# Sums of w_in in an earlier step, seven products in steps 5 and 18, and one filler less: a windowed attention and two-layer feed-forward kernel

## The chip, the core and the metric

The kernel runs on one core of one Trainium2 chip. The metric is the device time of an execution in microseconds (us); the number to be predicted is the median of the changed kernel's runs. A core has five engines with a queue each, worked in order: TensorE (PE: matmuls and, beside them, weight loads, PEld), VectorE (DVE), ScalarE (ACT), GpSimd (POOL) and SyncE (SP). They wait for each other by semaphores. Matmuls write to banks of PSUM, from where DVE or ACT take the results; everything else lies in SBUF. POOL issues the loads of q, k and v, SP the stores and the transposing DMAs.

## The reference

Eight batches and eight heads of 576 tokens with 64 channels: attention in a window of 32 tokens on either side, then a feed-forward block with a quick-GELU over all 4608 tokens of 512 channels.

```python
scores = scale * np.matmul(q, k.transpose(0, 1, 3, 2))
mask = np.abs(pos[:, None] - pos[None, :]) <= window          # window = 32
scores = np.where(mask, scores, -1000000000.0)
scores = scores - np.max(scores, axis=-1, keepdims=True)
attn = np.exp(scores)
attn = attn / (np.sum(attn, axis=-1, keepdims=True) + 1e-09)
attn_out = np.matmul(attn, v)
x = attn_out.transpose(0, 2, 1, 3).reshape(B * S, H * D)      # 4608 x 512
h = x @ w_in                                                  # 512 x 2048
g = h * (1.0 / (1.0 + np.exp(-1.702 * h)))
out = g @ w_out                                               # 2048 x 512
```

## The kernel before, in words

**Units and tiles.** The 4608 tokens, shifted by 32, are cut into 36 units of 128. For a unit u, `scores` makes the scores of 128 queries against the keys of their windows in 64 x 64 blocks (48 short matmuls) and lets ACT take the exponential; `band` multiplies with the 0/1 mask on DVE; `values` multiplies with v (and a column of ones, which gives the sums); `norm` divides on DVE; `x_T` transposes the result by a DMA on SP's queue into `xT`. Two units make a tile t of 256 tokens, `xT[t]`, on which the feed-forward block works.

**First layer, plain.** `layer1(t, d)` is a piece of two blocks of 128 of the 2048 hidden channels: 8 matmuls that stream 256 tokens each, into one bank, which ACT turns into `g` by its GELU. Eight pieces make the layer. A piece d above 3 covers blocks d and d + 8.

**First layer by seven products.** For half of the hidden channels (blocks 4 to 7 and 12 to 15) the product of a 2 x 2 block matrix can be made with seven block products instead of eight (Strassen's scheme in Winograd's form). `seven(t, n)` is one of them: 8 matmuls that stream 128 tokens each. It takes sums of blocks of x (`x_sums`, DVE) and of w_in (`w_in_sums`, DVE, made once), and collects in two banks, `h_main` and `h_side`; `move` copies or adds partial results between banks and SBUF (DVE or ACT), and `gelu` makes `g` of them.

**Second layer by seven products.** From tile 3 on g @ w_out goes the same way: `product(t, n)` is 8 matmuls that stream 256 columns, `g_sums` makes the sums of blocks of g (DVE), `w_sums` those of w_out (once, in the head). Products 1, 6, 7 and 4 add into one bank one after the other; after 1, 6 and 7 `keep` copies the running value to SBUF (DVE), and the next of them may not begin before. `result` adds the pieces to an output block, `store` sends it off.

**Order.** The program is an order written out by hand, engine queue by engine queue; nothing is reordered later, but for weight loads. It has five parts:

- `head`: loads, the first units, tiles 0 to 2. At its start PE gets *fillers*, matmuls on zeros whose result nobody reads (`keep_busy`). The number that is changed stands behind `blind(3)`, in front of the scores of units 2 and 3.
- `window(4)`: units 7, 8, 9, rest of the plain second layer, plain first layer of tile 3, all g sums of tile 3's first half, `feed(4)`.
- `window(5)`: units 10 and 11, products of tile 3, plain first layer of tile 4; at its end all g sums of tile 4's first half, `feed(5)`, the four w_in sums, and the last four pieces.
- `steady(w)` for w = 6 to 17: units 2w and 2w + 1, products of tile w - 2, first layer of tile w - 1 with four plain pieces and seven products. From w = 7 on, g sums 2 and 3 of a tile's first half are made in the step of its products (`if w > 6`).
- `window(18)` and `window(19)`, which go to `close`: no units are left. 18 interleaves the products of tile 16 with the plain first layer of tile 17; 19 has the products of tile 17 alone.

In the prediction "step w" is the part with that number. `loads(w)` stands at the head of a step and issues on POOL's queue the loads of v and of rows of q and k for later steps. `feed(w)` copies v for the odd blocks on DVE (`odd_v`), and issues four transposing DMAs of q and k rows (`rows_X`) on SP's queue. `gelu_table` brings ACT's table back to the GELU after the exponentials.

Banks: two of kind `h` (plain pieces; `h_main` and `h_side`), two of kind `b`, one each of `o` and `t`, and `a`, a pair of banks.

Of the kernel before, what the change touches and what calls it, by code (L numbers as in the profile page):

```python
# [15 lines left out]
F32 = mybir.dt.float32  # L16
# [11 lines left out]
class _Kernel:  # L28
# [454 lines left out]
    def head(self):  # L483

        nc, dve, act, pool = self.nc, self.nc.vector, self.nc.scalar, self.nc.gpsimd
# [55 lines left out]
        self.x_T(1, "o", dve)  # L541
        self.rest_T("q", "th", (dve, act))
        self.blind(3)
        self.keep_busy(2, "o")
        self.scores(2)
        self.scores(3)
        self.odd_v(2, dve)
# [23 lines left out]
        l2 = [(lambda c=c, u=u: self.layer2(u, c, "hhot"[u], (dve, act)[u % 2])) for c in range(4) for u in range(4)]  # L571

        def run(n):
            for _ in range(n):
                l2.pop(0)()

        run(4)
        for hp in range(4):
            self.rows_T("k", 1, hp, "b", dve)
            self.rows_T("q", 1, hp, "b", act)  # L580
            run(1)
        self.scores(4)
        self.scores(5)
        for m in range(4, 6):
            self.odd_v(m, dve)
        self.band(4)
        run(3)
        self.band(5)
        run(1)
# [43 lines left out]
        for c in "kq":  # L633
            self.rows_X(c, 3, (0, 1))

    def w_in_sums(self):

        w, ws, dve = self.w_in_sb, self.wi_sum, self.nc.vector
        top, low, u, v = slice(0, 2), slice(2, 4), slice(512, 1024), slice(1536, 2048)
        dve.tensor_add(ws[:, 0], w[:, top, v], w[:, low, v])  # L640
        dve.tensor_sub(ws[:, 1], ws[:, 0], w[:, top, u])
        dve.tensor_sub(ws[:, 2], w[:, top, u], w[:, top, v])
        dve.tensor_sub(ws[:, 3], w[:, low, u], ws[:, 1])

    def x_sums(self, t, which):

# [53 lines left out]
    def steady(self, w):  # L700

        dve, act = self.nc.vector, self.nc.scalar
        a, b, t, o = 2 * w, 2 * w + 1, w - 1, w - 2
        self.loads(w)
        self.scores(a, which=0)
        self.scores(b, which=1)
        self.g_sums(o, 1, (0, 1))
        self.product(o, 1, "o")
        self.keep(o, 1, dve)
        if w > 6:  # L710
            self.g_sums(o, 0, (2,))
        self.product(o, 2, "t")
        self.result(o, 11)
        self.gelu_table()
        self.product(o, 6)
        self.band(a)
        self.keep(o, 6, dve)
        self.product(o, 5, "t")
        self.band(b)
        self.g_sums(o, 1, (2,))  # L720
        self.seven(t, 1)
        self.move("side", "main", dve)
        self.x_sums(t, (0, 1))
        self.values(a, which=0)
        self.values(b, which=1)
        self.norm(a)
        self.x_T(a)
        self.product(o, 7)
        self.keep(o, 7, dve)
        self.result(o, 22)  # L730
        self.x_sums(t, (2, 3))
        self.norm(b)
        self.x_T(b)
        if w > 6:
            self.g_sums(o, 0, (3,))
        self.g_sums(o, 1, (3,))
        self.seven(t, 2)
        self.gelu(t, "side", 0, 0)
        self.seven(t, 6)
        self.move("k2", "main", act)  # L740
        self.layer1(t, 0, "a")
        self.product(o, 4)
        self.result(o, 21, act)
        self.seven(t, 7)
        self.move("k7", "side", act)
        self.seven(t, 5)
        self.move("22", "main", dve, "k7")
        self.feed(w)
        self.layer1(t, 1, "b")
        self.gelu(t, "22", 1, 1)  # L750
        self.layer1(t, 2, "b")
        self.layer1(t, 3, "a")
        self.seven(t, 4)
        self.move("21", "side", dve, "k2")
        self.seven(t, 3)
        self.gelu(t, "main", 0, 1)
        self.gelu(t, "21", 1, 0)
        self.g_sums(t, 0, (0, 1))
        self.product(o, 3)
        self.result(o, 12)  # L760

    def window(self, w):
        nc, dve, sp = self.nc, self.nc.vector, self.nc.sync
        a, b = 2 * w, 2 * w + 1
        att = w < self.NW
        t, act = w - 2, nc.scalar
        l1 = [(lambda d=d: self.layer1(w - 1, d)) for d in range(8)] if w <= self.NW else []

        def run(lst, n=1):
            for _ in range(min(n, len(lst))):  # L770
                lst.pop(0)()

        if w == 4:
            l2 = [(lambda u=u, i=i: self.layer2(u, i, "oh"[u % 2], (dve, act)[u % 2])) for u in (4, 5) for i in range(4)]
            self.scores(7)
            self.scores(a)
            run(l2, 3)
            self.band(7)
            self.scores(b)
            run(l2)  # L780
            self.band(a)
            self.values(7, "th")
            self.gelu_table()
            self.band(b)
            self.norm(7)
            run(l2, 2)
            self.values(a)
            self.values(b)
            run(l2)
            self.x_T(7, "t", nc.scalar)  # L790
            self.norm(a)
            self.x_T(a)
            self.norm(b)
            self.x_T(b)
            run(l2)
            self.loads(w)
            for m in (10, 11):
                self.odd_v(m, dve)
            run(l1, 8)
            self.g_sums(w - 1, 0)  # L800
            self.feed(w)
            return
        self.loads(w)
        if not att:
            self.close(w, l1)
            return
        self.scores(a, which=0)
        self.g_sums(t, 1, (0, 1))
        self.product(t, 1, "o")
        self.keep(t, 1, dve)  # L810
        self.product(t, 2, "h")
        self.scores(b, which=1)
        self.g_sums(t, 1, (2, 3))
        self.result(t, 11)
        self.gelu_table()
        self.product(t, 5, "t")
        self.band(a)
        self.product(t, 6)
        self.keep(t, 6, dve)
        self.band(b)  # L820
        run(l1)
        self.values(a, which=0)
        self.values(b, which=1)
        self.norm(a)
        self.x_T(a)
        self.product(t, 7)
        self.keep(t, 7, dve)
        self.result(t, 22)
        run(l1, 1)
        self.product(t, 4)  # L830
        self.result(t, 21, act)
        self.norm(b)
        self.x_T(b)
        self.product(t, 3)
        self.result(t, 12)
        run(l1, len(l1) - 4)
        self.g_sums(w - 1, 0)
        self.feed(w)
        self.w_in_sums()
        run(l1, 4)  # L840

    def close(self, w, l1):

        dve, act, t = self.nc.vector, self.nc.scalar, w - 2
        last = not l1
        if not last:
            self.g_sums(t, 0, (2, 3))
        self.g_sums(t, 1, (0, 1))
        for n, kind in ((1, "o"), (2, "b"), (6, None), (5, "b"), (7, None)):
            self.product(t, n, kind)  # L850
            if n in (1, 6, 7):
                self.keep(t, n, dve)
            if n == 1:
                self.g_sums(t, 1, (2, 3))
            if n == 2:
                self.result(t, 11)
            if l1:
                l1.pop(0)()
        self.result(t, 22)
        while len(l1) > 1:  # L860
            l1.pop(0)()
        if l1:
            self.g_sums(w - 1, 0)
        if not last:
            self.product(t, 4)
            self.result(t, 21, act)
            l1.pop(0)()
            self.product(t, 3)
            self.result(t, 12)
        else:  # L870
            both = self.work.tile([128, self.DM // 2], F32, name="part", tag="part", bufs=4)
            dve.tensor_add(both, self.part[t, "c"], self.part[t, 6])  # L872
            self.product(t, 3, "b")
            self.part[t, 6], self.part[t, "c"] = both, self.part[t, "d"]
            self.result(t, 12)
            self.product(t, 4)
            self.result(t, 21, act)

    def feed(self, w):

# [14 lines left out]

    def run(self):
        self.head()
        for w in range(4, self.NW + 2):
            self.steady(w) if 5 < w < self.NW else self.window(w)


@with_exitstack
# [44 lines left out]
```

The softmax here doesn't subtract the row's maximum and nothing guards it: scores larger than these inputs give would overflow.

## Time and profile before

| | us |
|---|---|
| median of 6 runs (288.22 to 291.67) | 289.13 |
| the profiled execution | 288.22 |
| its span, first to last instruction | 286.3 |
| PE busy | 278.1 |
| DVE busy | 217.1 |
| ACT busy | 193.3 |
| step 5 (scores of unit 10 to scores of unit 12) | 14.85 |
| step 6 | 15.60 |
| a steady step later on | 14.21 |
| step 18 | 13.10 |

The profile is of one execution. Its rows give start, duration, engine, line, operation, tile written and read, and how often; what stands in brackets at the end is how long the engine had idled and who let it go. `L119` is a helper that makes all copies, so a copy is told by the tile it writes: `part` is `keep`, `o_sb` an output block. `L437` are the products, `L375` the plain first layer, `L673` the seven products of the first layer. A table by stretch gives length, then busy time of each engine (with the number of instructions), PE's granted clock and the DMA load.

### The profile page before, as it was taken

To read this page: it belongs to the slowest core of one execution; us is meant where nothing else is said; L and a number is where in the kernel's file an instruction comes from. 1 tells how busy PE (TensorE), PEld (TensorE's weight loads), DVE (VectorE), ACT (ScalarE), POOL (GpSimd) and SP (SyncE) were. 2 spreads that over 40 slices of the span, in tenths; PEclk is the share of its full clock that TensorE was granted. 3 is DMA by queue.
4 is the path that set the end of the run, shared out by engine and by line. 5 is a ranking of instruction groups with operands and counts; after the bars stand their busy time and mean duration, and the time that the engine had idled before them with its cause. 6 is when DMAs were issued, how large, how long until landed. Compare 5 with 4: busy or idle time off the path is not lost.

```text
span 286.3 us, 9622 instructions
## 1 busy us (share of the span) xinstructions
PE 278.1 (97%) x4045; PEld 234.5 (82%) x4047; DVE 217.1 (76%) x586; ACT 193.3 (68%) x307; POOL 102.0 (36%) x140
## 2 busy tenths in 40 slices
PE   7989999999999899999999999999999999999994
PEld 2668665866888799999999999999999999999884
DVE  7771557778476979898979898979797979896452
ACT  4576467695766677777777777777777777776330
POOL 8864424997537262524343534332000000000000
PEclk9999999999999999999999999999999999999999
DMA  9999999999999999999999999999924321212012
GB/s 152 188 198 205 200 183 162 174 118 124 195 145 166 156 151 164 159 158 166 171 112 157 176 161 154 146 159 142 142 68 109 82 68 51 67 53 62 36 73 74
DMA packets 144827, 38.83 MB, mean 136 GB/s; under 512 B 129936, under 2 KB 140432, under 8 KB 144784
## 3 DMA queue, kind: packets, MB, share of 16 engines
q0 software_dynamic: 97232, 18.16, 87.4%
q1 hardware_dynamic: 47104, 19.67, 40.4%
q8 instruction: 31, 0.51, 0.8%
q10 hardware_dynamic: 448, 0.39, 0.5%
q14 instruction: 12, 0.10, 0.1%
HBM read 36.96 MB, written 9.44 MB: 162 GB/s over the span
## 4 chain that ended last, share of the span: by engine, by line
PE 65%; DVE 1%; ACT 0%; issue 0%; DVEq 0%
PE o_ps L437 30%; PE h_ps L375 17%; PE h_main L673 7%; PE h_side L673 6%; PE pv L326 3%; PE sc L287 2%; DVE o_sb L455 0%; DVE part L119 0%; ACT o_sb L119 0%; DVE part L872 0%; DVEq L455 0%
## 5 line engine op out<-in xcount | busy, mean ns | idle before, releaser
L375 PE MATMUL h_ps<-xT,w_in_sb 128*128 128x256 f16 x768 | 91.1, 273 | 0.0
L375 PEld LDWEIGHTS <-w_in_sb 128*128 128x128 f16 x768 | 73.7, 98 | 8.4
L377 ACT ACTIVATE g<-h_ps 128x512 f16<-128x512 f32 x96 | 57.1, 596 | 34.3 <-PE h_ps L375 32.6
L173 POOL DMA_DIRECT2D ve<-in_v_dram x41 | 34.4, 848 | 71.3 <-PE pv L326 53.7
L437 PEld LDWEIGHTS <-gs 128*128 128x128 f16 x480 | 45.3, 98 | 6.9 <-issue 1.4
L437 PE MATMUL o_ps<-w_sum,gs 128*128 128x256 f16 x360 | 44.3, 273 | 1.2 <-DVE part L119 1.2
L437 PEld LDWEIGHTS <-g 128*128 128x128 f16 x360 | 34.2, 98 | 4.3
L437 PE MATMUL o_ps<-w_out_sb,g 128*128 128x256 f16 x240 | 28.9, 273 | 0.0
L119 DVE COPY part<-o_ps 128x256 f32<-128x256 f32 x45 | 18.8, 419 | 10.2 <-PE o_ps L437 10.1
L119 DVE COPY vo<-ve 64x528 bf16<-64x528 bf16 x71 | 23.5, 331 | 3.7 <-DMA ve<-in_v_dram 1.7
L161 POOL DMA_DIRECT2D qs<-in_q_dram x27 | 22.8, 867 | 8.1 <-DMA ks<-in_k_dram 7.4
L161 POOL DMA_DIRECT2D ks<-in_k_dram x27 | 22.7, 856 | 3.9 <-DMA ve<-in_v_dram 3.3
L307 DVE TENSOR_TENSOR p<-p,mask 128x1024 bf16<-128x1024 bf16 x32 | 22.2, 695 | 2.6 <-ACT p L297 2.2
L673 PEld LDWEIGHTS <-wi_sum 128*128 128x128 f16 x384 | 23.5, 98 | 0.3
L387 PE MATMUL o_ps<-w_out_sb,g 128*128 128x512 f16 x96 | 23.2, 380 | 0.0
L455 DVE TENSOR_TENSOR o_sb<-o_ps,part 128x256 f32<-128x256 f32 x45 | 19.0, 422 | 5.5 <-PE o_ps L437 3.5
L688 ACT ACTIVATE g<-h_side 128x512 f16<-128x512 f32 x12 | 7.2, 597 | 21.0 <-DVE x L337 21.0
L295 ACT ACTIVATE p<-sc 128x512 bf16<-128x512 f32 x36 | 19.5, 597 | 1.9 <-PE sc L287 1.9
L673 PEld LDWEIGHTS <-w_in_sb 128*128 128x128 f16 x288 | 19.1, 98 | 0.8
L474 ACT ACT_TABLE_LOAD x15 | 19.2, 1283 | 0.3
L297 ACT ACT_TABLE_LOAD x15 | 19.2, 1283 | 0.3
L297 ACT ACTIVATE p<-sc 128x1024 bf16<-128x1024 f32 x18 | 18.5, 1025 | 1.4 <-PE sc L287 1.2
(105 smaller groups left out, 426.3 us busy)
## 6 DMA issues: line engine op xcount, KB each, us to landing
out_dram<-o_sb SPq DMA_DIRECT2D x34, 256.0 KB, 3.3
ve<-in_v_dram POOLq DMA_DIRECT2D x31, 128.0 KB, 6.3
ks<-in_k_dram POOLq DMA_DIRECT2D x24, 128.0 KB, 7.4
qs<-in_q_dram POOLq DMA_DIRECT2D x24, 128.0 KB, 9.2
w_in_sb<-in_moe_w_in_dram POOLq DMA_DIRECT2D x4, 512.0 KB, 8.6
w_out_sb<-in_moe_w_out_dram POOLq DMA_DIRECT2D x4, 512.0 KB, 13.6
ve<-in_v_dram POOLq DMA_DIRECT2D x10, 64.0 KB, 5.9
ks<-in_k_dram POOLq DMA_DIRECT2D x7, 64.0 KB, 6.0
```

The lines of the kernel that those rows point to most:

```text
L119: (eng.copy if eng is self.nc.scalar else eng.tensor_copy)(out, in_)
L161: self.nc.gpsimd.dma_start(self.stage[key][off:off + m, n], src[b, :, s:s + m, :].rearrange("h s d -> s h d"))
L173: self.nc.gpsimd.dma_start(self.ve[m % NV][lo + off:lo + off + n, :, :self.D], self.v[b, :, s:s + n, :].rearrange("h s d -> s h d"))
L295: nc.scalar.activation(p[:, eo], sc[eo], AF.Exp, scale=self.scale)
L297: nc.scalar.activation(p.rearrange("k e h s -> k e (h s)"), both, AF.Exp, scale=self.scale)
L307: self.nc.vector.tensor_mul(pv, pv, msk.to_broadcast([128, 8, 2, SQ]))
L375: nc.tensor.matmul(hps[:, i, :], self.w_in_sb[:, kr, ff * 128:(ff + 1) * 128], self.xT[t][:, kr, :], start=(i == 0 and kr == 0), stop=(i = ...
L377: nc.scalar.activation(self.g[t][:, ffs[0]:ffs[1] + 1:ffs[1] - ffs[0], :], hps, AF.Gelu_apprx_sigmoid)
L387: nc.tensor.matmul(o_ps, self.g[t][:, ff, s * 128:(s + 1) * 128], self.w_out_sb[:, ff, :], start=(ff == 0), stop=(ff == self.NFF - 1))
L437: nc.tensor.matmul(self.part[t, key], x, y, start=(first and k == 0), stop=(k == 7), skip_group_check=True)
L474: self.nc.scalar.activation(self.spark, self.spark, AF.Gelu_apprx_sigmoid)
L673: self.nc.tensor.matmul(dst[:, f], a, b, start=(n in (1, 7) and f == 0 and k == 0), stop=(f == 3 and k == 1), skip_group_check=True)
```

## The change

Four edits, of which the first two hang together.

1. `w_in_sums` takes a list of the sums to make. It is called in `window(4)` now: sums 0 and 1 before the first layer of tile 3, sums 2 and 3 after `feed(4)`.
2. `steady` runs for w = 5 too, so units 10 and 11 and the first layer of tile 4 go by the steady order: both score groups first, first layer with four plain pieces and seven products, `feed` earlier, g sums 2 and 3 of tile 4's first half in step 6 (`if w > 5`). The old branch of `window` for it is gone.
3. `steady` runs for w = 18 as well, with all that belongs to units left out and the plain piece 0 of tile 17 at an earlier place, piece 1 in the place of piece 0. So the first layer of tile 17 goes by seven products, and its g sums 2 and 3 of the first half move to `close`, which is left with the products of tile 17 alone; there all four g sums 2 and 3 stand between keep 1 and keep 6.
4. `head`: one filler instead of two behind `blind(3)`.

```diff
         self.blind(3)
-        self.keep_busy(2, "o")
+        self.keep_busy(1, "o")
         self.scores(2)
...
-    def w_in_sums(self):
+    def w_in_sums(self, which):
...
-        dve.tensor_add(ws[:, 0], w[:, top, v], w[:, low, v])
-        dve.tensor_sub(ws[:, 1], ws[:, 0], w[:, top, u])
-        dve.tensor_sub(ws[:, 2], w[:, top, u], w[:, top, v])
-        dve.tensor_sub(ws[:, 3], w[:, low, u], ws[:, 1])
+        for n in which:
+            x, y = [(w[:, top, v], w[:, low, v]), (ws[:, 0], w[:, top, u]),
+                    (w[:, top, u], w[:, top, v]), (w[:, low, u], ws[:, 1])][n]
+            (self.nc.vector.tensor_sub if n else self.nc.vector.tensor_add)(ws[:, n], x, y)
...
     def steady(self, w):
...
-        self.loads(w)
-        self.scores(a, which=0)
-        self.scores(b, which=1)
+        units = w < self.NW
+        if units:
+            self.loads(w)
+            self.scores(a, which=0)
+            self.scores(b, which=1)
         self.g_sums(o, 1, (0, 1))
         self.product(o, 1, "o")
         self.keep(o, 1, dve)
-        if w > 6:
+        if w > 5:
             self.g_sums(o, 0, (2,))
...
-        self.norm(b)
-        self.x_T(b)
-        if w > 6:
+        if units:
+            self.norm(b)
+            self.x_T(b)
+        else:
+            self.layer1(t, 0, "a")
+        if w > 5:
             self.g_sums(o, 0, (3,))
         self.g_sums(o, 1, (3,))
         self.seven(t, 2)
         self.gelu(t, "side", 0, 0)
         self.seven(t, 6)
         self.move("k2", "main", act)
-        self.layer1(t, 0, "a")
+        self.layer1(t, 0 if units else 1, "a" if units else "b")
...
-        self.feed(w)
-        self.layer1(t, 1, "b")
+        if units:
+            self.feed(w)
+            self.layer1(t, 1, "b")
         self.gelu(t, "22", 1, 1)
...
     def window(self, w):
...
         for m in (10, 11):
             self.odd_v(m, dve)
-        run(l1, 8)
+        self.w_in_sums((0, 1))
+        for d in range(8):
+            self.layer1(w - 1, d)
         self.g_sums(w - 1, 0)
         self.feed(w)
-        self.w_in_sums()
-        run(l1, 4)
+        self.w_in_sums((2, 3))
...
-    def close(self, w, l1):
+    def close(self):
...
         for n, kind in ((1, "o"), (2, "b"), (6, None), (5, "b"), (7, None)):
             self.product(t, n, kind)
             if n in (1, 6, 7):
                 self.keep(t, n, dve)
             if n == 1:
-                self.g_sums(t, 1, (2, 3))
+                self.g_sums(t, 0, (2,))
+                self.g_sums(t, 1, (2,))
             if n == 2:
                 self.result(t, 11)
-            if l1:
-                l1.pop(0)()
+                self.g_sums(t, 0, (3,))
+                self.g_sums(t, 1, (3,))
         self.result(t, 22)
...
     def run(self):
         self.head()
-        for w in range(4, self.NW + 2):
-            self.steady(w) if 5 < w < self.NW else self.window(w)
+        self.window(4)
+        for w in range(5, self.NW + 1):
+            self.steady(w)
+        self.close()
```

More of the change, by code (lines that the diff above doesn't have):

```diff
@@ L634, in head @@
             self.rows_X(c, 3, (0, 1))
-    def w_in_sums(self):
-        w, ws, dve = self.w_in_sb, self.wi_sum, self.nc.vector
+    def w_in_sums(self, which):
+        w, ws = self.w_in_sb, self.wi_sum
         top, low, u, v = slice(0, 2), slice(2, 4), slice(512, 1024), slice(1536, 2048)
[L640 to L643, printed above, removed]
+        for n in which:
+            x, y = [(w[:, top, v], w[:, low, v]), (ws[:, 0], w[:, top, u]),
+                    (w[:, top, u], w[:, top, v]), (w[:, low, u], ws[:, 1])][n]
+            (self.nc.vector.tensor_sub if n else self.nc.vector.tensor_add)(ws[:, n], x, y)
     def x_sums(self, t, which):
@@ L713, in steady @@
         self.result(o, 11)
-        self.gelu_table()
+        if units:
+            self.gelu_table()
         self.product(o, 6)
-        self.band(a)
+        if units:
+            self.band(a)
         self.keep(o, 6, dve)
         self.product(o, 5, "t")
-        self.band(b)
+        if units:
+            self.band(b)
         self.g_sums(o, 1, (2,))
@@ L723, in steady @@
         self.x_sums(t, (0, 1))
[L724 to L727, printed above, removed]
+        if units:
+            self.values(a, which=0)
+            self.values(b, which=1)
+            self.norm(a)
+            self.x_T(a)
         self.product(o, 7)
@@ L731, in steady @@
         self.x_sums(t, (2, 3))
-        self.norm(b)
-        self.x_T(b)
-        if w > 6:
+        if units:
+            self.norm(b)
[3 more added lines that the diff above has]
+        if w > 5:
             self.g_sums(o, 0, (3,))
@@ L747, in steady @@
         self.move("22", "main", dve, "k7")
-        self.feed(w)
-        self.layer1(t, 1, "b")
+        if units:
+            self.feed(w)
+            self.layer1(t, 1, "b")
         self.gelu(t, "22", 1, 1)
@@ L762, in window @@
     def window(self, w):
-        nc, dve, sp = self.nc, self.nc.vector, self.nc.sync
+        dve, act = self.nc.vector, self.nc.scalar
         a, b = 2 * w, 2 * w + 1
-        att = w < self.NW
-        t, act = w - 2, nc.scalar
-        l1 = [(lambda d=d: self.layer1(w - 1, d)) for d in range(8)] if w <= self.NW else []
         def run(lst, n=1):
@@ L771, in run @@
                 lst.pop(0)()
[L773 to L798, printed above, removed]
-            run(l1, 8)
-            self.g_sums(w - 1, 0)
-            self.feed(w)
-            return
@@ L803, in window @@
[L803 to L812, printed above, removed]
-        self.g_sums(t, 1, (2, 3))
-        self.result(t, 11)
+        l2 = [(lambda u=u, i=i: self.layer2(u, i, "oh"[u % 2], (dve, act)[u % 2])) for u in (4, 5) for i in range(4)]
+        self.scores(7)
+        self.scores(a)
@@ L815, in window @@
+        run(l2, 3)
+        self.band(7)
+        self.scores(b)
+        run(l2)
+        self.band(a)
+        self.values(7, "th")
         self.gelu_table()
[L816 to L819, printed above, removed]
         self.band(b)
-        run(l1)
-        self.values(a, which=0)
-        self.values(b, which=1)
+        self.norm(7)
+        run(l2, 2)
+        self.values(a)
+        self.values(b)
+        run(l2)
+        self.x_T(7, "t", act)
@@ L824, in window @@
         self.norm(a)
         self.x_T(a)
[L826 to L831, printed above, removed]
         self.norm(b)
         self.x_T(b)
-        self.product(t, 3)
-        self.result(t, 12)
-        run(l1, len(l1) - 4)
+        run(l2)
+        self.loads(w)
+        for m in (10, 11):
+            self.odd_v(m, dve)
+        self.w_in_sums((0, 1))
+        for d in range(8):
+            self.layer1(w - 1, d)
@@ L837, in window @@
         self.g_sums(w - 1, 0)
         self.feed(w)
-        self.w_in_sums()
-        run(l1, 4)
-    def close(self, w, l1):
[L844 to L847, printed above, removed]
+        self.w_in_sums((2, 3))
+    def close(self):
+        dve, act, t = self.nc.vector, self.nc.scalar, self.NW - 1
         self.g_sums(t, 1, (0, 1))
@@ L853, in close @@
             if n == 1:
-                self.g_sums(t, 1, (2, 3))
+                self.g_sums(t, 0, (2,))
+                self.g_sums(t, 1, (2,))
             if n == 2:
                 self.result(t, 11)
-            if l1:
-                l1.pop(0)()
+                self.g_sums(t, 0, (3,))
+                self.g_sums(t, 1, (3,))
         self.result(t, 22)
[L860 to L877, printed above, removed]
+        both = self.work.tile([128, self.DM // 2], F32, name="part", tag="part", bufs=4)
+        dve.tensor_add(both, self.part[t, "c"], self.part[t, 6])
+        self.product(t, 3, "b")
+        self.part[t, 6], self.part[t, "c"] = both, self.part[t, "d"]
+        self.result(t, 12)
+        self.product(t, 4)
+        self.result(t, 21, act)
     def feed(self, w):
```

## The prediction

> **What bounds the kernel now.** I read the page's totals first, then the table of busy time by stretch, the chain that ended last, the waits, and the queues of VectorE (DVE) and TensorE (PE) around the edits. All times are microseconds from the span's start.
>
> ```profile
> span 286.3 us, 9622 instructions
> PE 278.1 (97%) x4045; PEld 234.5 (82%) x4047; DVE 217.1 (76%) x586; ACT 193.3 (68%) x307; POOL 102.0 (36%) x140
> 76.50:91.35 14.85, 14.85 (x201) 12.83 (x200) 9.70 (x26) 9.82 (x15) 7.14 (x9) 1.00 1.89 164
> 91.35:106.95 15.60, 14.37 (x225) 12.84 (x224) 13.57 (x35) 10.95 (x18) 7.86 (x10) 1.00 1.94 155
> 106.95:121.16 14.21, 14.21 (x225) 12.85 (x224) 12.42 (x34) 10.73 (x18) 5.74 (x7) 1.00 1.99 159
> 263.15:276.25 13.10, 13.10 (x122) 11.74 (x120) 6.16 (x17) 5.60 (x10) 0.00 (x0) 1.00 0.08 29
> ```
>
> The last four rows are steps 5, 6, 7 and 18: length, then busy time of PE, weight loads, DVE, ACT, POOL, and the granted clock, which is 1.00 everywhere. PE is busy without a break in steps 5, 7 and 18, so each is as long as its matmuls. Step 6 alone loses 15.60 - 14.37 = 1.23 to idling. It has the same work as step 7, but is 15.60 - 14.21 = 1.39 longer (the idle time and the PE's refill). The waits name the culprit, and DVE's queue explains it:
>
> ```profile
> PE o_ps L437 <- DVE part L119: 1.2, 1, 1.2
> 91.36 0.68 DVE L640 TENSOR_TENSOR wi_sum<-w_in_sb 128x1024 f16<-128x1024 f16 x1
> 92.07 0.69 DVE L641 TENSOR_TENSOR wi_sum<-wi_sum,w_in_sb 128x1024 f16<-128x1024 f16 x1
> 92.68 0.68 DVE L642 TENSOR_TENSOR wi_sum<-w_in_sb 128x1024 f16<-128x1024 f16 x1
> 93.28 0.68 DVE L643 TENSOR_TENSOR wi_sum<-w_in_sb,wi_sum 128x1024 f16<-128x1024 f16 x1
> 94.68 0.42 DVE L119 COPY part<-o_ps 128x256 f32<-128x256 f32 x1
> 95.15 1.91 PE L437 MATMUL o_ps<-w_sum,gs 128*128 128x256 f16 x16 [1.23 <-DVE part L119]
> ```
>
> The four sums of w_in hold DVE from 91.36 to 93.88. The two g sums and the copy that saves product 1 (keep 1) stand behind them, and product 6 may not add into the same bank before keep 1 ends at 95.10.
>
> **Sums one step sooner.** The four cost 93.88 - 91.36 = 2.52 of DVE wherever they stand; the question is the cover. In window 4 DVE shows two gaps:
>
> ```profile
> 73.75 0.42 DVE L414 TENSOR_TENSOR gs<-g 128x512 f16<-128x512 f16 x1 [2.83 <-ACT g L377]
> 77.24 0.42 DVE L414 TENSOR_TENSOR gs<-g 128x512 f16<-128x512 f16 x1 [1.47 <-ACT g L377]
> ```
>
> Sums 0 and 1 (1.32 until the next may start) fall into the 2.83 before 73.75. Sums 2 and 3 follow the ring copies that end at 75.77: two starts 0.60 apart and 0.68 of run, so they end near 77.0, ahead of the g sum that waits until 77.24 for ACT. The margin there is 0.2. Without that cover, keep 1 of step 5 comes late: its product 1 ends about 78.2, so another 0.2 are free, and after that product 6 at 78.88 waits. I take 0 for the placing (bounds 0 and +0.5), and -1.39 for step 6, which becomes the row of step 7.
>
> **Step 5 by seven products.** A plain first-layer piece is 8 matmuls of 256 columns, a seven-product is 8 of 128 columns; the chain of step 7 gives both:
>
> ```profile
> 114.22 0.87 PE h_ps L375 x8
> 115.09 0.87 PE o_ps L437 x8
> 115.96 0.45 PE h_side L673 x8
> ```
>
> Four pieces (4 x 0.873 = 3.49) become seven products (7 x 0.447 = 3.13): -0.36. The two score groups now run together, and values follow seven 1, so there are fewer changes between 64-row and 128-row matmuls, 0.093 each in the starts of PE (six in step 5 before, four in step 7). The whole difference is read directly: 14.85 - 14.21 = **-0.64**.
>
> Here the Trainium skill speaks against the change. "TensorE: Matmul & The Clock Gate", section "Back-to-back issue gap", gives about 81 ns per matmul for streams of weight load and 128-column matmul. This trace has 8 in 0.45, 56 ns each, weight loads included, in twelve steps. With 81 ns seven products cost 56 x 0.081 = 4.54, +1.05 instead of -0.36, and over steps 5 and 18 the forecast would be 2.8 worse. The row is of the very instructions that are added, so I take it.
>
> Does step 5 stall where step 7 doesn't? Its first g sums wait for ACT until 77.24, so ACT's table load and exponentials run 0.35 late against the steady steps. I walked DVE's queue with the gaps of the steady rows (0.34 for a 256-column operation or a g sum, 0.60 for a mask or move): keep 1 ends 78.65 (product 6 due 78.88); mask of unit 10 at 79.58; keep 6 at 80.19; mask of unit 11 at 80.57, because ACT's exponential ends 80.52; third g sum done 81.6 (product 7 due 81.8); normalization of unit 10 done about 83.56 (its bank is wanted at 83.58). Everything arrives, the last with nothing to spare: +0.05, bounds 0 and +0.4. Step 5 leaves out two g sums that later steps have, which lets DVE catch up.
>
> What moves with the step: feed (four copies of v on DVE, 1.26, and four transposing DMAs on SP, 6.2 of SP's time) now stands ahead of three first-layer pieces. On DVE it starts near 87.3 instead of 90.17, in time that steady steps have free; on SP near 87.6 instead of 88.52. The loads it needs were issued by 72.6 and landed within 14.5 at most (median 9.2), 87.1. Loads on POOL's queue keep their place at the head of the step.
>
> **Step 18 and the close.** (Times on the clock of before, so that only differences count.) Step 18's matmuls are 7 x 0.873 + 4 x 0.873 + 7 x 0.447 = 12.73 instead of 13.10. But plain pieces no longer stand between products 1, 2 and 6. DVE: result 12 at 263.44, g sums at 263.77 and 264.22, keep 1 at 264.56 to 264.98; product 6, due at 264.91, starts at 265.03: 0.12 lost. The close therefore starts at 276.01 instead of 276.26. Its DVE queue is longer than now:
>
> ```profile
> 277.59 0.42 DVE L119 COPY part<-o_ps 128x256 f32<-128x256 f32 x1
> 279.13 0.42 DVE L119 COPY part<-o_ps 128x256 f32<-128x256 f32 x1
> 280.88 0.42 DVE L119 COPY part<-o_ps 128x256 f32<-128x256 f32 x1 [1.32 <-PE o_ps L437]
> ```
>
> These are keep 1, keep 6 and keep 7. The same pattern as in step 18 puts keep 1 at 277.41 and product 6 at 277.88. Between keep 1 and keep 6 then stand five operations (four g sums, result 11) instead of three: 277.75, 278.09, 278.42, 278.76, 279.09, so keep 6 runs 279.43 to 279.85. Product 7, due at 279.63, starts at 279.90 and ends 280.77, against 280.68 now. So the step's 0.36 is given back: **+0.09** for the end (bounds -0.3 and +0.6).
>
> **One filler less.** The first filler starts 15.07, scores of unit 2 at 15.59: two fillers of 0.213 (one is missing in the records) and a change of 0.093. ACT's last query copy ends 15.22, so with one filler scores start at 15.38: **-0.21**. The exponentials and values after it waited for these scores, and PE shows no idling from 20.9 to 76.5 that would absorb it; if v copies on DVE (done 17.95) hold it instead, 0. PE idles 0.9 near 19 without losing pace, so I give the missing filler no price in clock.
>
> **Sum.** -1.39 - 0.64 + 0.05 + 0.09 - 0.21 = -2.10. The profiled execution took 288.22, 1.95 around its span of 286.27; it would take 286.1 and its span 284.2. Against the median of 289.13, which lies 0.91 above the profiled one, I predict **287.0**, -0.73%. A change under 0.5% (1.45) can hardly be told from none here.
>
> **Rivals.**
> 1. *The stall moves instead of going* (0.18): sums 2 and 3 run late, or step 5's queue of DVE has less slack than walked. For it: two margins of 0.2 or less, and DVE over 90% busy in every other slice of the page from step 6 on. Against it: later steps recover. Price 0.5 to 1.5: about 288.1, within 0.5%.
> 2. *Seven products at the page's pace* (0.03): 287.0 + 2.8 = 289.8, no measurable change.
> 3. *The close gives back more, and the filler nothing* (0.12): +0.6 and 0 in place of +0.09 and -0.21: 287.7, on the border of 0.5%.
> 4. *Slower, by late rows* (0.04): in window 4 SP once waited 7.7 for a key load before its transposes. If feed of step 5 meets this, the transposes of x queued behind it come late. In steady steps they stand on SP 6.9 after the scores, so near 97.7 in step 6; feed needs 6.2, so it may start as late as 91.4. Two transposes (3.4) and a landing (6.0) end at 107.1, and step 7 wants x 4.1 after its scores, near 109.1: another 2.0. Loads landing after 93.4 cost PE one for one; to end over +0.5% they must be 2.10 + 1.45 beyond that, near 97: 290.7. The longest landing seen ends at 87.1.
>
> **How the numbers follow.** The forecast has 0.63, its own range 286.4 to 287.6. Rival 1's middle and rival 3 fill the upper side, and the lower bounds of the close (-0.3) and of the spread of the runs (288.22 to 291.67 before) the lower one: 286.0 to 288.6 leaves out about 2 in 10. Faster by over 0.5%: the forecast, half of rival 3, a little of rival 1: 0.74. Within: 0.20. Slower: 0.06.
>
> **What would show it.** PE's wait for "part" at 95 is gone, step 6 lasts 14.2; step 5 starts its first seven product 4.1 after its scores and lasts 14.2 to 14.3; the w_in sums lie before 77.1; scores of unit 2 start at 15.4; in the close PE waits about 0.3 for keep 6 before product 7, and keep 7 stands 2.1 sooner than 280.88. A new PE wait in step 5, or transposes of rows waiting for a load near 88, would make it wrong.

## The result and the profile after

The changed kernel takes 286.3 us (median of 18 runs, 285.9 to 289.03), the kernel before 289.01 in the runs beside it (39 runs, 287.9 to 291.74). The ratio is 0.9911, with a 95% interval from 0.9891 to 0.9931: 2.6 us less (2.0 to 3.2), where 2.10 was forecast. One execution of the kernel of experiment 6 (290.03, at a mean granted clock of 0.988) was in the chip's slower state and is left out of the times below.

The profiled execution of the changed kernel is one of its longer ones (287.44). Its span is 285.7, almost the 286.3 of before. So spans of two single executions would have told little here. What has to be compared are stretches. The scores of unit 10 open step 5, at 76.51 before and at 77.95 after; this execution had lost 1.44 by then. Of that, 0.88 were lost near 20 us to a late load of w_in and 0.55 in window 4 to slow copies of v (both further down). The w_in sums stand in window 4 too, but they don't hold PE there: from the scores of unit 9 to those of unit 10 PE takes 13.24 in the kernel before and 13.23 in the second profile of the changed kernel. From the scores of unit 10 to the end the changed kernel takes 285.70 - 77.95 = 207.75, against 286.27 - 76.51 = 209.76: **2.01 less**. The table by stretch of the kernel after gives steps 5, 6 and 18, with columns as before:

```profile
77.95:92.19 14.24, 14.24 (x226) 12.84 (x225) 11.95 (x31) 10.96 (x18) 6.16 (x7) 1.00 2.07 146
92.19:106.40 14.21, 14.21 (x226) 12.84 (x226) 12.57 (x34) 10.73 (x18) 6.24 (x8) 1.00 1.83 162
262.59:275.45 12.86, 12.86 (x147) 11.74 (x145) 8.00 (x22) 5.84 (x12) 0.00 (x0) 1.00 0.12 43
```

Step 5 fell from 14.85 to 14.24, step 6 from 15.60 to 14.21, step 18 from 13.10 to 12.86, and PE is busy through steps 5 and 6. Product 6, before which PE had idled 1.23, now follows without idle time (nothing in brackets):

```profile
94.58 1.69 PE L437 MATMUL o_ps<-w_sum,gs 128*128 128x256 f16 x14
```

The DVE queue of the same kernel shows where the sums went (`L643` is their line now) and what cover is left in front of the g sums:

```profile
72.76 0.67 DVE L643 TENSOR_TENSOR wi_sum<-w_in_sb 128x1024 f16<-128x1024 f16 x1
73.46 0.69 DVE L643 TENSOR_TENSOR wi_sum<-wi_sum,w_in_sb 128x1024 f16<-128x1024 f16 x1
75.20 0.43 DVE L414 TENSOR_TENSOR gs<-g 128x512 f16<-128x512 f16 x1 [1.04 <-ACT g L377]
...
76.91 0.68 DVE L643 TENSOR_TENSOR wi_sum<-w_in_sb 128x1024 f16<-128x1024 f16 x1
77.51 0.68 DVE L643 TENSOR_TENSOR wi_sum<-w_in_sb,wi_sum 128x1024 f16<-128x1024 f16 x1
78.69 0.42 DVE L414 TENSOR_TENSOR gs<-g 128x512 f16<-128x512 f16 x1 [0.50 <-ACT g L377]
```

DVE idled 2.83 and 1.47 at these two places before; 1.04 and 0.50 are left. The sums cost nothing where they stand.

### The profile page after: what moved, and what is told of

Its sections match the earlier page's. It is cut to its first block, busy times and chain, and to the rows that moved or that the text cites. A ratio compares the mean times of both kernels' runs of the same rounds, so it can differ in the third digit from the quotient of the medians.

```text
span 285.7 us, 9735 instructions
## 1 busy us (share of the span) xinstructions
PE 278.1 (97%) x4093; PEld 234.7 (82%) x4094; DVE 224.9 (79%) x600; ACT 194.9 (68%) x311; POOL 102.1 (36%) x140
## 5 line engine op out<-in xcount | busy, mean ns | idle before, releaser
L375 PE MATMUL h_ps<-xT,w_in_sb 128*128 128x256 f16 x704 | 83.4, 273 | 0.7 <-DMA w_in_sb<-in_moe_w_in_dram 0.7
L375 PEld LDWEIGHTS <-w_in_sb 128*128 128x128 f16 x704 | 67.2, 98 | 8.5 <-DMA w_in_sb<-in_moe_w_in_dram 0.9
L377 ACT ACTIVATE g<-h_ps 128x512 f16<-128x512 f32 x88 | 52.2, 596 | 30.3 <-PE h_ps L375 28.3
L119 DVE COPY vo<-ve 64x528 bf16<-64x528 bf16 x71 | 26.8, 378 | 5.3 <-DMA ve<-in_v_dram 3.5
L673 PEld LDWEIGHTS <-wi_sum 128*128 128x128 f16 x448 | 27.4, 98 | 0.3
L673 PEld LDWEIGHTS <-w_in_sb 128*128 128x128 f16 x336 | 22.3, 98 | 0.9
L688 ACT ACTIVATE g<-h_side 128x512 f16<-128x512 f32 x14 | 8.4, 597 | 21.3 <-DVE x L337 18.3
L683 DVE TENSOR_TENSOR hs<-h_side,hs 128x512 f32<-128x512 f32 x14 | 9.7, 692 | 12.6 <-PE h_side L673 12.6
```

The source lines that it names most:

```text
L119: (eng.copy if eng is self.nc.scalar else eng.tensor_copy)(out, in_)
L375: nc.tensor.matmul(hps[:, i, :], self.w_in_sb[:, kr, ff * 128:(ff + 1) * 128], self.xT[t][:, kr, :], start=(i == 0 and kr == 0), stop=(i = ...
L377: nc.scalar.activation(self.g[t][:, ffs[0]:ffs[1] + 1:ffs[1] - ffs[0], :], hps, AF.Gelu_apprx_sigmoid)
L673: self.nc.tensor.matmul(dst[:, f], a, b, start=(n in (1, 7) and f == 0 and k == 0), stop=(f == 3 and k == 1), skip_group_check=True)
```

## The experiments

All were timed beside the kernel before. Since the time up to step 5 differs by up to 1.6 us between executions, the profile of each was cut in the same places. "To step 5" is the time from the span's start to the first scores of unit 10; "tail" is from the last scores (unit 34) to the end of the span. The two rows marked "again" are the kernels before and after themselves, in another profiled execution.

| kernel | median us | ratio to before (95%) | to step 5 | step 5 | step 6 | tail |
|---|---|---|---|---|---|---|
| before | 289.01 | 1 | 76.51 | 14.85 | 15.60 | 37.23 |
| before, again | 289.24 | 0.9994 (0.9971 to 1.0018) | 77.29 | 14.86 | 15.80 | 37.23 |
| sums alone | 287.64 | 0.9938 (0.9912 to 0.9964) | 77.88 | 14.86 | 14.23 | 37.20 |
| sums and step 5 | 286.58 | 0.9902 (0.9873 to 0.9932) | 77.02 | 14.32 | 14.20 | 37.13 |
| one filler alone | 289.0 | 1.0006 (0.9976 to 1.0035) | 76.56 | 14.85 | 15.99 | 37.20 |
| after | 286.3 | 0.9911 (0.9891 to 0.9931) | 77.95 | 14.24 | 14.21 | 37.23 |
| after, again | 286.42 | 0.9906 (0.9878 to 0.9934) | 76.63 | 14.24 | 14.20 | 37.23 |
| after without step 18 | 286.82 | 0.9914 (0.9885 to 0.9942) | 76.94 | 14.50 | 14.22 | 37.14 |
| after, close in other order | 286.3 | 0.9904 (0.9882 to 0.9926) | 76.36 | 14.34 | 14.21 | 36.99 |
| after, keeps on ACT | 286.56 | 0.9911 (0.9884 to 0.9938) | 77.63 | 14.23 | 14.21 | 36.73 |
| after, sums in a row | 286.78 | 0.9934 (0.9903 to 0.9964) | 77.42 | 14.78 | 14.20 | 37.25 |
| after, no filler | 286.47 | 0.9915 (0.989 to 0.994) | 76.48 | 14.24 | 14.21 | 37.22 |
| after, keeps on ACT, v copies later | 286.46 | 0.9902 (0.9868 to 0.9937) | 77.84 | 14.24 | 14.21 | 36.74 |

**1. The sums alone.** The kernel before, with `w_in_sums` called as in the changed kernel; everything else is old.

```diff
             for m in (10, 11):
                 self.odd_v(m, dve)
+            self.w_in_sums((0, 1))
             run(l1, 8)
             self.g_sums(w - 1, 0)
             self.feed(w)
+            self.w_in_sums((2, 3))
             return
...
         self.feed(w)
-        self.w_in_sums()
         run(l1, 4)
```

> The kernel before with one edit: the four sums of w_in stand in window 4 (two before the first layer of tile 3, two behind its feed), steps 5 and 18, close and the two fillers stay as they were. Theory: only the stall of step 6 goes, -1.39 us against the kernel before; step 6 falls from 15.60 to 14.2, step 5 stays at 14.85. Rival 1 (the stall moves instead of going): 0 to -0.9 us, with a wait of PE for the copy of product 1 in step 5 or 6.

Its table by stretch has steps 5 and 6 (this table and those of experiment 4 are cut 0.2 in front of a step's first scores):

```profile
77.68:92.54 14.86, 14.86 (x203) 12.80 (x200) 9.97 (x27) 9.82 (x16) 7.00 (x8) 1.00 1.91 156
92.54:106.77 14.23, 14.23 (x226) 12.84 (x224) 11.48 (x30) 10.79 (x19) 6.32 (x8) 1.00 1.83 162
```

Step 5 is as long as it was (14.86), step 6 is 14.23, and from step 5 to the end the kernel takes 286.25 - 77.88 = 208.37, 1.39 less than before. So the first rival falls for this placing of the sums: the stall goes and comes back nowhere. That this execution reached step 5 as late as 77.88 goes with its granted clock, which fell to half for 3.41 in the head, where the profile of before has 1.00:

```profile
8.31:11.72 3.41, 3.13 (x74) 2.25 (x75) 2.16 (x5) 2.34 (x5) 2.49 (x4) 0.50 1.43 193
```

**2. Sums and step 5.** The first kernel with step 5 by the steady order.

```diff
-            self.steady(w) if 5 < w < self.NW else self.window(w)
+            self.steady(w) if 4 < w < self.NW else self.window(w)
...
-        if w > 6:
+        if w > 5:
```

> The kernel before with the sums in window 4 and step 5 by the steady order with seven products; step 18, close and the two fillers as before. Theory: -1.39 - 0.64 + 0.05 = -1.98 us against the kernel before, step 5 at 14.2 to 14.3. Rival 1: step 5 stalls, -0.9 to -1.4. Rival 2 (81 ns for each matmul of 128 columns): -1.39 + 1.05 - 0.2 = -0.5.

From step 5 to the end 284.79 - 77.02 = 207.77: 1.99 less than before, 1.98 was expected. Step 5 lasts 14.32, 0.54 less than in the first kernel. The pace of rival 2 would have made it 0.8 longer.

**3. The change without step 18.** The second kernel with one filler, which is the changed kernel with the old step 18 and the old close.

```diff
-        self.keep_busy(2, "o")
+        self.keep_busy(1, "o")
         self.scores(2)
```

> The changed kernel with step 18 and close put back as before (plain first layer of tile 17 between the products). Theory: the edit of step 18 is worth +0.09 us to the end, so this kernel takes -2.19 us against the kernel before, 0.1 less than the changed kernel. If seven products in step 18 are worth their 0.36 to the end, it is 0.36 slower than the changed kernel, -1.74. Rival 3 (close gives back more): 0.6 faster than the changed kernel, -2.7.

Its tail is 37.14. Of all kernels, those with the plain step 18 have tails of 37.23, 37.23, 37.20, 37.13, 37.20 and 37.14 (mean 37.19), and those with the new step 18 and the close unchanged have 37.23, 37.23, 37.25 and 37.22 (mean 37.23). The tails of one order scatter by 0.1, but that scatter lies behind PE's work. PE's last product, of which the rows are from the kernels before and after, tells the orders apart:

```profile
281.55 1.04 PE L437 MATMUL o_ps<-w_sum,g 128*128 128x256 f16 x8
```

```profile
281.06 1.04 PE L437 MATMUL o_ps<-w_sum,g 128*128 128x256 f16 x8
```

It starts 32.51 after the scores of unit 34 (which start at 249.04 and 248.47) in all six kernels with the plain step 18, and 32.59 to 32.60 in the four with the new one. So step 18 by seven products costs 0.08 to 0.09 on PE, as forecast (+0.09), although the step itself fell from 13.10 to 12.86. The times (ratios 0.9914 and 0.9911) can't tell the two apart.

**4. One filler alone.** The kernel before with one line changed.

```diff
-        self.keep_busy(2, "o")
+        self.keep_busy(1, "o")
         self.scores(2)
```

> The kernel before with one filler instead of two in front of the scores of units 2 and 3, nothing else. Theory: scores of unit 2 start 0.21 us sooner after blind(3), -0.21 us. Rival 3: 0, because copies of v on VectorE or a load hold what follows. Its step 6 is also a second look at the stall: 1.39 us again if the wait for the sums has one size, another if it varies between executions.

No gain is seen, and 0.21 is too small for these intervals. Its step 6 told more. Its table by stretch has for step 6:

```profile
91.21:107.20 15.99, 14.37 (x227) 12.83 (x224) 14.50 (x35) 10.80 (x19) 6.50 (x9) 1.00 2.07 155
```

The four v copies of feed in DVE's queue, in the first profile of before:

```profile
90.17 1.26 DVE L119 COPY vo<-ve 64x528 bf16<-64x528 bf16 x4
```

The same copies with one filler, and in PE's queue the matmuls that wait:

```profile
90.23 1.65 DVE L119 COPY vo<-ve 64x528 bf16<-64x528 bf16 x4
95.58 0.60 PE L437 MATMUL o_ps<-w_sum,gs 128*128 128x256 f16 x4 [1.62 <-DVE part L119]
```

The second profile of the kernel before, by stretch and then in the same queues:

```profile
91.95:107.75 15.80, 14.37 (x227) 12.83 (x224) 14.06 (x35) 10.80 (x19) 6.28 (x8) 1.00 2.08 157
```

```profile
90.96 1.45 DVE L119 COPY vo<-ve 64x528 bf16<-64x528 bf16 x4
96.13 0.38 PE L437 MATMUL o_ps<-w_sum,gs 128*128 128x256 f16 x2 [1.43 <-DVE part L119]
```

> The kernel before without an edit, another profile. Theory: step 6 has its stall, 1.4 us plus what the four copies of v in front of the sums of w_in run over 1.26 us. If the stall has one size whatever the copies take: 1.4.

The four v copies of feed stand in front of the sums. They took 1.26 and 1.45 in the two profiles of before and 1.65 in this one, and step 6, whose order is the same in all three, took 15.60, 15.80 and 15.99. The stall has no fixed size: it is 1.39 plus what the copies run over, since DVE was the path there.

**5. The close in another order.** The changed kernel, g sums 3 behind keep 6.

```diff
             if n == 2:
                 self.result(t, 11)
+            if n == 6:
                 self.g_sums(t, 0, (3,))
                 self.g_sums(t, 1, (3,))
```

> The changed kernel with g sums 3 of the close behind keep 6 instead of in front of it. Theory: keep 6 starts as soon as product 6 has ended, PE's gap of 0.26 us before product 7 goes, -0.26 us against the changed kernel (-2.36 against the kernel before). If the gap has another cause, 0.

The products 6, 5 and 7 of the close are one row of 24 matmuls in PE's queue. First the changed kernel, PE's queue and then DVE's, with keep 1, the four g sums and result 11 between, and keep 6:

```profile
277.32 3.04 PE L437 MATMUL o_ps<-w_sum,gs 128*128 128x256 f16 x24
```

```profile
276.85 0.42 DVE L119 COPY part<-o_ps 128x256 f32<-128x256 f32 x1
277.18 0.75 DVE L418 TENSOR_TENSOR gs<-g 128x512 f16<-128x512 f16 x2
277.85 0.42 DVE L455 TENSOR_TENSOR o_sb<-o_ps,part 128x256 f32<-128x256 f32 x1
278.19 0.75 DVE L420 TENSOR_TENSOR gs<-g,gs 128x512 f16<-128x512 f16 x2
278.85 0.41 DVE L119 COPY part<-o_ps 128x256 f32<-128x256 f32 x1
```

The same two queues with the g sums behind keep 6:

```profile
276.21 2.78 PE L437 MATMUL o_ps<-w_sum,gs 128*128 128x256 f16 x24
```

```profile
275.74 0.42 DVE L119 COPY part<-o_ps 128x256 f32<-128x256 f32 x1
277.28 0.42 DVE L119 COPY part<-o_ps 128x256 f32<-128x256 f32 x1
```

The row is 0.26 shorter, because keep 6 comes 1.54 behind keep 1 instead of 2.00. The tail falls from 37.23 to 36.99.

**6. Keeps on ScalarE.** The changed kernel; `units` is false in step 18 alone.

```diff
-        self.keep(o, 1, dve)
+        self.keep(o, 1, dve if units else act)
...
             if n in (1, 6, 7):
-                self.keep(t, n, dve)
+                self.keep(t, n, act if n < 7 else dve)
```

> The changed kernel with the copies keep 1 and keep 6 of the close and keep 1 of step 18 on ScalarE, which has nothing to do at these places, instead of VectorE. Theory: all three gaps of PE at the end go (0.12 in step 18, 0.13 before product 6 and 0.26 before product 7 in close), -0.51 us against the changed kernel (-2.61 against the kernel before). If the g sums and not the copies hold product 6, only the 0.26 goes.

ACT's queue in the close, with keep 1 and keep 6. In brackets is the idle time before each, and what ended it:

```profile
276.50 0.37 ACT L119 COPY part<-o_ps 128x256 f32<-128x256 f32 x1 [0.63 <-PE o_ps L437]
278.31 0.37 ACT L119 COPY part<-o_ps 128x256 f32<-128x256 f32 x1 [1.43 <-PE o_ps L437]
```

Both waited for nothing but PE's own product. The tail is 36.73, 0.50 less than in the changed kernel, and PE runs through step 18 and the close without a gap. The gaps of the changed kernel there add up to the same (0.13 in step 18, 0.13 and 0.26 in the close), so all of the loss at the end came from the place of these copies in DVE's queue. The times can't show it: the median is 286.56, over five runs from 285.46 (the lowest of all kernels) to 287.02.

**7. Sums in a row.** The changed kernel with the cover of sums 0 and 1 taken away.

```diff
-        self.w_in_sums((0, 1))
...
-        self.w_in_sums((2, 3))
+        self.w_in_sums((0, 1, 2, 3))
```

> The changed kernel with all four sums of w_in behind feed of window 4, so that sums 0 and 1 lose the cover of the 2.83 us gap in VectorE's queue. Theory: keep 1 of step 5 ends about 0.67 us after product 6 is due, PE waits that long there and nowhere else, +0.67 us against the changed kernel (-1.43 against the kernel before). If the place in window 4 doesn't matter: 0.

Step 5 has the wait again, at the place that was named (keep 1 in DVE's queue, product 6 in PE's):

```profile
79.91 0.42 DVE L119 COPY part<-o_ps 128x256 f32<-128x256 f32 x1
80.38 0.82 PE L437 MATMUL o_ps<-w_sum,gs 128*128 128x256 f16 x6 [0.40 <-DVE part L119]
```

Step 5 is 14.78, 0.54 longer than in the changed kernel (0.67 expected). So half of the sums cost 0.54 in the wrong one of two places in the same window, and nothing in the right one.

**8. No filler.** The changed kernel without the call behind `blind(3)`.

```diff
-        self.keep_busy(1, "o")
         self.scores(2)
```

> The changed kernel without the last filler too. Theory: scores of unit 2 then wait for ScalarE's query copy alone and start 0.1 us sooner, -0.1 us against the changed kernel (-2.2 against the kernel before). If the fillers keep up PE's pace, matmuls from 15 to 20 us run slower and the time rises by 0.5 us or more.

Scores of unit 2 start at 15.29, 0.32 after the second matmul of `blind(3)`; two fillers gave 0.84 in the profile of before, one gave 0.53 in that of after. The scores now wait for the query copies of DVE and ScalarE, so the first layer starts 1.08 after that matmul, against 1.16 in the profile of after: 0.08 sooner, near the 0.1 expected. The 16 first-layer matmuls behind keep their pace (1.92 in all three). The time is that of the changed kernel within the interval, so neither the 0.1 nor a loss of pace is seen.

**9. Keeps on ScalarE and v copies later.** In window 4, the copies of v for units 8 and 9 stand behind the mask of unit 7. The reason was a loss of PE before the values of unit 7, 0.24 to 0.56 in four of the other twelve profiles (last section).

```diff
-        for m in (7, 8, 9):
-            self.odd_v(m, dve)
+        self.odd_v(7, dve)
...
         self.band(7)
+        for m in (8, 9):
+            self.odd_v(m, dve)
         self.scores(b)
```

> The changed kernel with the copies keep 1 and keep 6 at the end on ScalarE, and in window 4 the copies of v for units 8 and 9 behind the mask of unit 7 instead of in front of it on VectorE. Theory: the end is 0.5 us shorter as before with these copies on ScalarE, and PE's wait of about 0.6 us before the values of unit 7, seen in some executions where six copies of v ran slow, goes or shrinks: -0.5 to -0.8 us against the changed kernel. If the slow copies only move the wait to units 8 and 9: -0.5.

The tail is 36.74 again. But the four copies now hold up the masks of units 8 and 9 and the copy of an output block; in its profile they took 2.58, and PE lost 0.75 and 0.32 at the values of window 4. The wait only moved, and grew. No version is clearly below the changed kernel in its time.

**The changed kernel again.**

> The changed kernel without an edit, beside the other two on the same chip. Theory: from the scores of unit 10 to the end 207.7 to 208.0 us again, the same as in its first profile; the time up to these scores differs from execution to execution by up to 1.5 us. If the changed kernel's gain is in the head too, that time is shorter than in the kernel before.

From step 5 to the end it takes 284.38 - 76.63 = 207.75, the same as in its first profile, while the time up to step 5 is 1.32 shorter. So the gain sits behind step 5's first scores, and the spread in front of them.

## Why the prediction was right

- **What bounds the kernel.** Right. Where PE idled, time could be had, and it was had; where PE was busy, only fewer matmul cycles helped.
- **Sums one step sooner, -1.39.** Right in place and, for the profile it was read from, in size: the first experiment has 1.39. As a figure for the median it was too small. The copies in front of the sums belong to the stall; the three profiles have 1.39, 1.59 and 1.78, the mean of which is 1.59. One profile gave one draw of a varying term.
- **Step 5, -0.64 + 0.05.** Right: 14.85 to 14.24, -0.61. The row (8 seven-product matmuls in 0.45, 56 ns each) held, now in two more steps, against the 81 ns per matmul that "TensorE: Matmul & The Clock Gate" of the Trainium skill gives in its section "Back-to-back issue gap"; the measurement decides. In three of the other kernels step 5 lasted 14.32 to 14.50 instead, with a gap of 0.11 to 0.30 inside seven-product 2, at which the profile shows no engine that PE waits for. It isn't peculiar to step 5: one later step each lasts 14.56 in experiment 5 and 14.64 in experiment 6, instead of 14.21, with such a gap. Its cause is open.
- **Step 18 and the close, +0.09.** Right in every step: product 6 of step 18 waited 0.13 (0.12 forecast), product 6 of the close 0.13, product 7 0.26 (0.27), and the step's saving was given back. PE's last product comes 0.08 to 0.09 later. Experiments 5 and 6 take the waits away by their cause.
- **One filler less, -0.21.** The step was right for the scores and wrong for what follows. In every profile with fillers here, scores start 0.52 after the first of two and 0.31 after a single one: the 0.21 is there. But in the first profile of after the first layer then waited for its load of w_in:

```profile
20.68 0.50 PE L375 MATMUL h_ps<-xT,w_in_sb 128*128 128x256 f16 x3 [0.72 <-DMA w_in_sb<-in_moe_w_in_dram]
```

The forecast looked for idling of PE from 20.9 on that could absorb the gain, and saw the copies of v as the one thing in front; the load was ready in the profile of before, where these matmuls started at 19.80, and not in this one. The filler itself can also start late, since it writes a bank that a DVE copy must leave first: it began 0.22 to 0.55 after the second `blind(3)` matmul. Kernels with two fillers reach step 5 at 76.51, 77.02, 77.29 and 77.88 (mean 77.18; 76.94 without the last, which had the half clock), those with one at 76.36 to 77.95 (mean of eight 77.17), the one with none at 76.48. What a filler is worth to the end stays open.
- **Rivals.** Rival 1's margins were real (taking away part of the cover costs 0.54), but they held. Rival 2 fell with step 5. Rival 3 came in half at most: no gain by the filler was seen, but the close gave back no more than forecast. Rival 4 did not come: no transpose of rows is late enough to hold PE in steps 5 to 7.
- **The sum.** -1.39 - 0.61 + 0.00 is -2.00 in the two profiles, and 2.01 was measured there. The times say 2.6 (2.0 to 3.2). The mean stall explains 0.2 of the rest; whether the remaining 0.4 is a real gain or lies in the interval isn't settled. The median of 286.3 is 0.7 below the 287.0 that was forecast: just under the forecast's own range (286.4 to 287.6), inside the wider one (286.0 to 288.6). If the filler is worth nothing, its -0.21 stood in for a stall that was put 0.20 too small, and that part of the agreement is luck.

## What to carry to other kernels

Where one engine is busy nearly all the time, look for the one place in which it isn't, follow its wait to the queue in front, and move what stands there into an idle stretch of that queue; count the cover in front of the next wait before and after. Saving matmuls in a step is worth nothing if the copies that separate them become the path: when work between two dependent products goes, check what freed the bank in between, and which idle engine could do that. Compare kernels by stretches between the same two events, since the part in front can differ between executions (here by 1.6) by most of what the change is worth.

## What the runs showed of the hardware that was not expected

A copy of v (64 partitions x 528, DVE) takes 0.289 to 0.296 in all eleven copies after 210 us, when POOL issues no loads. Earlier it takes up to 0.87. Six of them stand in front of window 4; the rows are from the kernels before and after:

```profile
59.68 2.37 DVE L119 COPY vo<-ve 64x528 bf16<-64x528 bf16 x6
```

```profile
60.58 4.84 DVE L119 COPY vo<-ve 64x528 bf16<-64x528 bf16 x6
65.34 0.67 DVE L307 TENSOR_TENSOR p<-p,mask 128x1024 bf16<-128x1024 bf16 x1
```

In the second, the mask of unit 7 comes 1.4 later, counted from the scores of unit 9, and PE loses 0.55 to it. In the profile of after, the 27 copies that POOL's issue of a load covers for more than 30% of their time take 0.507 in the mean, and the 41 without any overlap 0.300; in that of before 0.398 (22) and 0.301 (48). All thirteen profiles have this order, but not every covered copy is slow: 11 of the 27 take 0.30 or less. This goes with "SBUF — State Buffer" of the Trainium skill, section "SBUF: two separate sides": DVE in certain modes and GpSimd share one pair of ports, of which the loser waits for the other's whole instruction. The page warns that DVE holds up POOL's loads; here the traces show the copies growing instead. That these copies run in such a mode is not shown by any run here. It is a coincidence in time, not an experiment: no kernel took POOL's issues away, and two slow copies in the profile of before (0.42 and 0.59) have no issue beside them. Whatever makes them slow, slow copies are what made the stall of step 6 vary, and part of what makes executions of one kernel differ by 3 to 4 us. The granted clock is another part: of the 17 executions of the kernel before that ran beside experiments 5 to 8, three had a mean clock of 0.993 to 0.995 and spans of 288.0 to 289.2, the other 14 a median span of 287.15.
